# A two-part kernel on one core: another order of the first loads, and two score levels of the first unit in one product

## The chip, the cores and the metric

The kernel runs on one core of one Trainium2 chip. The metric is the device time of one execution in microseconds (us). The engines are PE (TensorE: matmuls, with PEld its weight loads), DVE (VectorE), ACT (ScalarE), POOL (GpSimd) and SP (SyncE, which here only issues DMAs).

## The reference

A recurrent attention with a decaying state feeds a mixture of four experts. All is float32.

```python
# q, k, v, alpha: (B, H, S, D) = (4, 8, 768, 48)
state = zeros(B, H, D, D)
for t in range(S):
    state = alpha[:, :, t, :, None] * state + einsum('bhd,bhe->bhde', k[:, :, t], v[:, :, t])
    y[:, :, t] = einsum('bhd,bhde->bhe', q[:, :, t], state)
x = y.transpose(0, 2, 1, 3).reshape(3072, 384)
# w1: (4, 384, 1024), w2: (4, 1024, 384), domain_probs: (3072, 4)
p = domain_probs / (domain_probs.sum(-1, keepdims=True) + 1e-9)
for e in range(4):
    out += p[:, e:e+1] * (maximum(x @ w1[e], 0) @ w2[e])
```

## The kernel before

**Units and groups.** The attention is cut into 24 units: one batch entry and 128 time steps, all 8 heads. Units are gathered into groups of two (the first) or four, and a group's 256 or 512 tokens go through the experts. The work on the experts (`up`: x times w1; `down`: the hidden layer times w2) is written out group by group and expert by expert; the generators of the attention units are stepped in between by a list of due times. The order on each engine is that of the code: the schedule is manual.

**Scores by levels.** Within a unit, the score of a query at step t with a key at an earlier step s needs the product of alpha over s+1 to t. This is done by seven levels: level li has blocks of m = 2^li steps and pairs the second half of each block pair (queries) with the first (keys). Between levels, `next_q(li)` (DVE) multiplies the queries of the second halves by the decay of the first half, `same_q(li)` (ACT) copies the others; `next_k(li)` and `same_k(li)` do the like for keys, whose first halves get the decay of the second half. `dec(li)` multiplies neighbouring decays. `QTs[li]` and `KTs[li]` are the queries and keys as level li needs them; `QTs[0]` is the query times alpha of its own step.

**The first unit** has a function of its own, `first_unit`, since nothing lies beside it. `turned` transposes an input by four TensorE products with an identity (a float32 product runs as two passes, and shows as two matmuls). `products(li, outs)` multiplies, for 4 head pairs, 2 heads and 2 halves of 64 keys, 64 keys by the 32 level-li queries of the half: 16 products. `take` (DVE) copies the masked scores of a level into `diag`. `fill` issues products with zeros into a bank that nobody reads. The tiles `QTs[1:]`, `KTs`, `plain` and `diag` lie in the buffers of the w1 pieces of later groups (`places`); the inputs of unit 1 (`apart`) and the decays lie in `spare`, which is the first of four buffers named `hT`. The other `hT` buffers are unused until `up` takes all four as `hidden`, the hidden layer of the first expert; before that, the four pieces of that expert's w2 are loaded into them.

**The first loads.** SP issues in the order of the code: unit 0's alpha, q, k, v; unit 1's alpha, k, q, v; the four pieces of the first expert's w1 (lines 1028 and 1029); unit 2's alpha, k and q after level 3's keys (line 433), into the tiles that held unit 0's; the probabilities `p_all` after the first unit (line 1043), in rows of 16 bytes; at the first `up` (line 805) the four pieces of w2; right after, four pieces of w1 and four of w2 of the second expert (lines 815 to 818 and 806). A tile that held something else waits for its readers, and each issue also waits for the eighth DMA before it to be done.

Of the kernel before, what the change touches and what calls it, by code (L numbers as in the profile page):

```python
# [10 lines left out]
F32 = mybir.dt.float32  # L11
F32R = mybir.dt.float32r
# [8 lines left out]
def kernel(  # L21
# [37 lines left out]
    nc = tc.nc  # L59
# [244 lines left out]
    def halves(t, m):  # L304
        return t.rearrange("p a (b two r) -> p a b two r", two=2, r=m)
# [7 lines left out]
    def first_unit(fill, other):  # L313
# [7 lines left out]
                       for i in range(3 * KC * QF // (NP * P))]  # L321
        place_of = iter(places)
        AT = work.tile([P, NP, P], F32, name="AT")
        QTs = [work.tile([P, NP, P], F32, name="QT")] + [next(place_of) for _ in range(6)]
        KTs = [next(place_of) for _ in range(7)]
        plain = next(place_of)
        diag, later_half = (next(place_of).rearrange("p a (i n) -> p (a i) n", i=2) for _ in range(2))
# [16 lines left out]
        def same_q(li):  # L344
            old, new = (used(t, li) for t in QTs[li:li + 2])
            nc.scalar.copy(out=new[:, :, :, 0, :], in_=old[:, :, :, 0, :])  # L346
# [25 lines left out]
        def products(li, outs):  # L372
            each = QUAD // LEVELS[li]
            qv = halves(QTs[li], LEVELS[li])
            scored(outs, KTs[li], lambda p, i, s: qv[rows[i], p, each * s:each * (s + 1), 1, :])

        def take(li, outs):
            for i in range(2):
                to = diag[:, NP * i:NP * (i + 1)]
                if li < 0:  # L380
                    nc.vector.copy_predicated(
                        to, masks_all[:, 6 * QUAD:6 * QUAD + HALF].unsqueeze(1).broadcast_to([P, NP, HALF]), outs[i])
                    continue
                m = LEVELS[li]
                mk = masks[:, li, :].rearrange("p (b r) -> p b r", r=m)
                nc.vector.copy_predicated(
                    to.rearrange("p a (b two r) -> p a b two r", two=2, r=m)[:, :, :, 1, :],
                    mk.unsqueeze(1).broadcast_to([P, NP, QUAD // m, m]),
                    outs[i].rearrange("p a (b r) -> p a b r", r=m))
# [6 lines left out]
        tq = turned(pair(rq))  # L396
        dec(0)
        nc.vector.tensor_mul(QTs[0], tq, AT)
        same_q(0)
        next_q(0)  # L400
        tk = turned(pair(rk))
        nc.scalar.copy(out=KTs[0], in_=tk)
        same_q(1)
        same_k(0)
        dec(1)
# [3 lines left out]
        fill(1, DM)  # L409
        fill(1)  # L410
        first = two("sc", HALF, tag="sc")
        products(0, part(first, 0))
        tq = turned(pair(rq))
        same_q(2)
        next_q(2)
        same_k(1)
        next_k(1)
        products(1, part(first, QUAD))
        same_q(3)
        for li in (3, 4, 5):  # L420
            dec(li)
# [8 lines left out]
        same_q(4)  # L430
        next_k(3)
        same_k(3)
        load(2, "akq")
        products(3, part(second, QUAD))
        take(0, part(first, 0))
        same_q(5)
# [358 lines left out]
    def up(gi, e, fc, slots=None):  # L795
        n = len(groups[gi]) * P
        lo, hi = (slots.start * P, slots.stop * P) if slots else (0, n)
        begins, ends = lo == 0, hi == n
        c, f = divmod(fc, FPQ)
        i = first_piece(gi, e) + c  # L800
        if fc == 0 and begins:
            for k in range(NQ):
                hidden[k] = hid.tile([P, 2, FPQ, NT], F32R, name="hT", bufs=NQ)
        if gi == fc == 0 and begins and e != 1:
            for k in range(NQ):
                load_piece(1, e * NQ + k, beside=True)
        beside = BESIDE[(gi, e) == (1, 0)]
        if fresh(gi, e) and fc in beside and begins:
            making.append(split_piece(1, first_piece(gi, e) + beside[fc]))
        if gi == 0 and e > 0 and fc in SPLIT_AT:  # L810
            making.append(split_piece(0, e * NQ + SPLIT_AT[fc]))
        if gi == 0 and e == E - 1 and fc in (3, 6):
            making.append(split_piece(1, E * NQ + 1 + fc // 3))
        if gi == 0 and e + 1 < E and fc == FCH // 2 and begins:
            for k in range(NQ if e + 1 < E - 1 else 0):
                load_piece(0, (e + 1) * NQ + k)
            for k in range(NQ if e == 0 else 0):
                load_piece(1, NQ + k, beside=True)
        col = slice(f * P, (f + 1) * P)
        if gi > 0:  # L820
            w = wt[0][i].rearrange("p t (c f) -> p t c f", f=QF)[:, :, :, col]
        else:
            w = wt[0][i].rearrange("p (c f) -> p c f", f=QF)[:, :, col]
        parts = [hidden[c][:, part, f, lo:hi] for part in range(2)]
        whole = parts[1].bitcast(F32)
        one = ps.tile([P, NT], F32, name="one", tag="g", bufs=4)[:, :hi - lo]
        if gi == 0:
            for kc in range(KC):
                nc.tensor.matmul(one, lhsT=w[:, kc], rhs=xraws[gi][:, kc, lo:hi],  # L829
                                 start=(kc == 0), stop=(kc == KC - 1))  # L830
            nc.scalar.activation(out=whole, in_=one, func=ACT.Relu)
        else:
            for part in (1, 2, 0):
                for kc in range(KC):
                    nc.tensor.matmul(one, lhsT=w[:, (0, 2, 1)[part], kc], rhs=x_part(gi, part % 2, kc)[:, lo:hi],  # L835
                                     start=(part == 1 and kc == 0), stop=(part == 0 and kc == KC - 1))
            nc.scalar.activation(out=parts[0], in_=one, func=ACT.Relu)  # L837
            while finish:
                hidden_rest(*finish.popleft())
            finish.append((one, parts))  # L840
        while finish and fc == FCH - 1:
            hidden_rest(*finish.popleft())
        background()
        if f == FPQ - 1 and ends:
            if gi == 0:
                for k in range(2 if e == E - 2 and c > 1 else 0):
                    load_piece(0, (E - 1) * NQ + 2 * (c - 2) + k)
                for k in range(NQ if e == E - 2 and c == NQ - 1 else 0):
                    load_piece(1, E * NQ + k)
                for k in range(2 if e == E - 1 and c > 1 else 0):  # L850
                    load_piece(0, E * NQ + 2 * (c - 2) + k)
            elif gi != LAST - 1:
                del wt[0][i]
                load_piece(0, i + AHEAD)
            while late:
                load_piece(1, late.popleft(), rest=True)
            while stores:
                stores.popleft()()
# [154 lines left out]
    with tc.manual_schedule():  # L1013
# [11 lines left out]

        load(0, "aqkv")
        load(1, "akqv")
        for i in range(NQ):
            load_piece(0, i)

# [3 lines left out]
        def fill(times, n=P):  # L1036
            for _ in range(times):
                nc.tensor.matmul(idle[:, :n], lhsT=zeros[:, :P], rhs=zeros[:, :n], start=True, stop=True)  # L1038
# [1 line left out]
        runs = [None, attention(1), attention(2)]  # L1040
        fill(7)
        runs[0] = first_unit(fill, runs[1])
        nc.sync.dma_start(out=p_all, in_=moe_domain_probs.rearrange("(n p) e -> p n e", p=P))

        waiting.extend(sorted([*((at, 1, runs[1]) for at in
                                 (0.4, 1.0, 2.1, 3.1, 4.4, 6.0, 7.2, 8.2, 9.2, 9.9, 10.4, 10.5, 14.4)),
                               (13.5, 2, runs[2]),
# [59 lines left out]
```

## Time and profile before

| what | us |
| --- | --- |
| three runs | 966.0, 966.89, 967.09 (median 966.89) |
| the profiled execution | 965.53 |
| its span | 963.7 |
| PE busy in it | 954.8 |
| weight loads busy | 851.9 |
| DVE, ACT, POOL busy | 534.9, 419.0, 246.2 |
| first matmul of `up` starts | 20.55 |
| first matmul of `down` starts | 26.45 |

The span is from the first to the last instruction of the profiled execution, its own time is the same execution as the device counts it. In the profile, tiles are named as in the code, but by the buffer's name where tiles share one: `w` and `w2r` are weight buffers (the first unit's `QTs`, `KTs` and `diag` show as `w`, the first expert's w1 as `w2r` or a part of `w`), `hT` the four buffers told of above, `sa`, `sk`, `sq` the tiles of alpha, k and q of units 0 and 2, `rv` the values, `tp` a bank of transposes, `sc` and `near` banks of scores, `one` and `ops` banks of `up` and `down`. "PE sc L370 x32" is then 16 products into a score bank, written at line 370. "issue" in the chain is a time in which the engine waited for nothing that the profile shows.

### The profile page before, as it was taken

Reading aid. Unit: us, or ns where it says so; the run is one execution under the profiler, and the core shown is the slowest. Engines: PE = TensorE matmul, PEld = TensorE weight load, DVE = VectorE, ACT = ScalarE, POOL = GpSimd, SP = SyncE. Lnnn points to the kernel's source line nnn. Section 1 sums busy time; section 2 is a strip of 40 time slices with the busy share of each in tenths; the row PEclk is TensorE's granted clock in tenths of the full one; section 3 lists DMA queues with packets and bytes.
Section 4 is the critical chain, followed back from the end, with each engine's and each line's share of the span. In section 5 each row is a group of like instructions: output and inputs, shape, how many; then the busy total and the mean of one; then the engine's idle time right before and its main releaser. Section 6 shows DMA issues by size and latency. Waiting matters only on the chain.

```text
span 963.7 us, 24883 instructions
## 1 busy us (share of the span) xinstructions
PE 954.8 (99%) x10252; PEld 851.9 (88%) x10252; DVE 534.9 (56%) x1127; ACT 419.0 (43%) x975; POOL 246.2 (26%) x403
## 2 busy tenths in 40 slices
PE   8999999999999999999999999999999999999998
PEld 7777779898998988989989889898898899999998
DVE  5666897778588555655645456646764312221312
ACT  5786766536445444444344333555435222021111
POOL 3121332344245222313212223223221202020200
PEclk9999999999999999999999999999999999999999
DMA  9898999999899999999999899999998609192821
GB/s 198 269 298 272 308 304 252 265 334 295 214 356 322 317 309 300 250 326 303 289 308 266 270 284 321 335 252 292 298 297 263 230 1 350 44 326 68 297 97 50
DMA packets 215618, 251.21 MB, mean 261 GB/s; under 512 B 95281, under 2 KB 184753, under 8 KB 215505
## 3 DMA queue, kind: packets, MB, share of 16 engines
q1 hardware_dynamic: 160464, 164.74, 58.3%
q0 software_dynamic: 54592, 84.55, 30.2%
q8 instruction: 81, 1.33, 0.6%
q10 hardware_dynamic: 448, 0.32, 0.1%
q14 instruction: 33, 0.26, 0.1%
HBM read 219.69 MB, written 29.88 MB: 259 GB/s over the span
## 4 chain that ended last, share of the span: by engine, by line
PE 98%; ACT 1%; issue 0%; DVE 0%; POOL 0%; DVEq 0%; POOLq 0%; ACTq 0%
PE ops L914 43%; PE one L835 38%; PE one L829 4%; PE yps L712 4%; PE sc L591 4%; PE tp L310 2%; PE sc L667 1%; PE sps L752 1%; PE sc L672 1%; PE idle L1038 0%; ACT w L346 0%; POOL lat L690 0%; PE sc L370 0%; PE y L481 0%; ACT w L355 0%
## 5 line engine op out<-in xcount | busy, mean ns | idle before, releaser
L835 PE MATMUL one<-xT,w 128*128 128x512 f32 (+1 forms) x1512 | 343.1, 383 | 0.0
L835 PEld LDWEIGHTS one<-xT,w 128*128 128x128 f32 x1512 | 271.5, 188 | 53.0 <-DVE hT L862 0.4
L914 PE MATMUL ops<-w,hT 128*128 128x384 f32 x1408 | 254.2, 338 | 0.0
L914 PEld LDWEIGHTS ops<-w,hT 128*128 128x128 f32 x1408 | 243.2, 188 | 2.5 <-issue 0.2
L837 ACT ACTIVATE hT<-one 128x512 fp32r<-128x512 f32 (+1 forms) x200 | 108.7, 547 | 280.6 <-PE one L835 279.6
L862 DVE SCALAR_TENSOR_TENSOR hT<-one,hT 128x512 fp32r<-128x512 f32 (+1 forms) x200 | 124.7, 627 | 170.6 <-ACT hT L837 170.3
L223 POOL DMA_DIRECT2D w<-in_moe_w_dram x140 | 105.8, 757 | 377.8 <-PE one L835 276.2
L914 PE MATMUL ops<-w2r,hT 128*128 128x384 f32 x704 | 127.8, 337 | 0.0
L914 PEld LDWEIGHTS ops<-w2r,hT 128*128 128x128 f32 x704 | 122.1, 188 | 0.3 <-issue 0.2
L563 ACT COPY qb<-QT 64x256 f32<-64x256 f32 x230 | 92.5, 402 | 33.0 <-DVE QT L570 31.0
L570 DVE TENSOR_TENSOR QT<-QT,AT 128x256 f32<-128x256 f32 x158 | 71.8, 455 | 33.0 <-ACT qb L563 24.7
L935 DVE SCALAR_TENSOR_TENSOR acc<-ops,p_all,acc 128x384 f32<-128x384 f32 x66 | 39.6, 612 | 86.1 <-PE ops L914 86.0
L584 DVE TENSOR_TENSOR KT<-KT,AT 128x256 f32<-128x256 f32 x161 | 76.2, 473 | 0.0
L601 DVE COPY_PREDICATED near<-masks,sc 128x128 f32<-128x128 uint8 x115 | 40.9, 355 | 62.0 <-PE sc L591 60.2
L690 POOL COPY lat<-near 32x256 f32<-32x256 f32 x92 | 45.6, 496 | 87.3 <-DVE near L601 84.0
L583 ACT COPY KT<-KT 128x256 f32<-128x256 f32 x115 | 47.2, 411 | 4.7 <-PE sc L591 2.4
L554 ACT ACTIVATE odd<-QT,ident 64x256 f32<-64x256 f32 x36 | 18.8, 523 | 69.6 <-DVE QT L512 69.3
L572 DVE TENSOR_TENSOR AT<-AT 128x256 f32<-128x256 f32 (+1 forms) x138 | 42.2, 306 | 4.7
L762 POOL TENSOR_TENSOR st<-st,dec 64x192 f32<-64x192 f32 x32 | 17.1, 535 | 95.1 <-PE yps L712 93.9
L554 ACT ACTIVATE odd<-QT 64x256 f32<-64x256 f32 x46 | 20.1, 437 | 45.0 <-DVE QT L570 44.6
L835 PE MATMUL one<-KT,w 128*128 128x256 f32 x288 | 34.6, 279 | 0.0
L835 PEld LDWEIGHTS one<-KT,w 128*128 128x128 f32 x288 | 34.4, 188 | 0.0
(135 smaller groups left out, 895.8 us busy)
## 6 DMA issues: line engine op xcount, KB each, us to landing
w<-kept SPq DMA_DIRECT2D x80, 768.0 KB, 7.4
w<-in_moe_w_dram POOLq DMA_DIRECT2D x140, 384.0 KB, 8.6
w<-kept SPq DMA_DIRECT2D x60, 384.0 KB, 6.4
w2r<-kept SPq DMA_DIRECT2D x60, 384.0 KB, 7.6
kept<-w POOLq DMA_DIRECT2D x16, 768.0 KB, 6.3
raw<-in_moe_w_dram SPq DMA_DIRECT2D x24, 384.0 KB, 9.2
kept<-w POOLq DMA_DIRECT2D x16, 384.0 KB, 8.2
kept<-w2r POOLq DMA_DIRECT2D x16, 384.0 KB, 8.2
```

Of the source, the lines that this page charges most:

```text
L223: nc.gpsimd.dma_start(out=out.rearrange("p (c n) -> p c n", c=(KC, FPQ)[l]), in_=whole_piece(l, i))
L563: nc.scalar.copy(out=qb[rows, :, i, :].rearrange("p a (b r) -> p a b r", r=m), in_=qv[rows])
L570: nc.vector.tensor_mul(qv, qv, spread(dv[:, :, :, 0], m))
L572: nc.vector.tensor_mul(dec, dv[:, :, :, 0], dv[:, :, :, 1])
L583: nc.scalar.copy(out=new[:, :, :, 1, :], in_=old[:, :, :, 1, :])
L584: nc.vector.tensor_mul(new[:, :, :, 0, :], old[:, :, :, 0, :], spread(halved(decs[li])[:, :, :, 1], m))
L601: nc.vector.copy_predicated(near.rearrange("p a (b two r) -> p a b two r", two=2, r=m)[:, :, :, 1, :], mk.unsqueeze(1).broadcast_to([P, H, ...
L690: nc.gpsimd.tensor_copy(out=lat[rows, :, rows], in_=near[rows])
L835: nc.tensor.matmul(one, lhsT=w[:, (0, 2, 1)[part], kc], rhs=x_part(gi, part % 2, kc)[:, lo:hi], start=(part == 1 and kc == 0), stop=(part ...
L837: nc.scalar.activation(out=parts[0], in_=one, func=ACT.Relu)
L862: nc.vector.scalar_tensor_tensor(out=low, in0=x, scalar=0.0, in1=top.bitcast(F32), op0=ALU.max, op1=ALU.subtract)
L914: nc.tensor.matmul(sums[slot], lhsT=h, rhs=w, start=(n == begins[slot]), stop=(n == ends[slot]))
```

## The change

The first expert's w1 is no longer loaded right behind unit 1's values. `load(2, "a")` and pieces 0 and 1 are issued when unit 0's keys have been copied, then `load(2, "k")`; `load(2, "q")` and pieces 2 and 3 follow after level 3's keys. `p_all` is loaded behind the first expert's w2, in `up`. Of this w2, piece 3 is issued before piece 2.

The products of levels 0 and 1 become one. With `KTs[1]`, even keys carry the decay of the odd step after them, so that the level-0 score of an odd query is its product with the plain query, without its own alpha. `close_q` holds the plain odd queries (`odd_q`, a copy on ACT out of the transposes' bank) and `QTs[1]` side by side, and `close_products` multiplies 64 keys by 64 queries, 16 products, with the result where the two levels' scores were. `close_q` is the second `hT` buffer, so that `hidden` now begins at the third: `hidden[2]` is `spare`, `hidden[3]` is `close_q`. Where `products(0)` stood, a fill of 384 columns is issued.

```diff
-        QTs = [work.tile([P, NP, P], F32, name="QT")] + [next(place_of) for _ in range(6)]
+        close_q = hid.tile([P, 4, NT], F32R, name="hT", bufs=NQ).rearrange("p f n -> p (f n)")
+        close_q = close_q[:, :2 * NP * P].bitcast(F32).rearrange("p (l a n) -> p l a n", l=2, n=P)
+        QTs = [work.tile([P, NP, P], F32, name="QT"), close_q[:, 1]] + [next(place_of) for _ in range(5)]
...
+        def odd_q(tq):
+            of = tq.rearrange("p a (b r two) -> p a b r two", r=2, two=2)[:, :, :, :, 1]
+            nc.scalar.copy(out=halves(close_q[:, 0], 2)[:, :, :, 1, :], in_=of)
+
+        def close_products(outs):
+            for p in range(NP):
+                for i in range(2):
+                    for s in range(2):
+                        rhs = close_q[rows[i], :, p, keys[s]].rearrange("q l (b two r) -> q l b two r", two=2, r=2)
+                        to = outs[i][keys[s], p].rearrange("q (l b r) -> q l b r", l=2, r=2)
+                        nc.tensor.matmul(to, lhsT=KTs[1][rows[i], p, keys[s]], rhs=rhs[:, :, :, 1, :],
+                                         start=True, stop=True)
...
         nc.vector.tensor_mul(QTs[0], tq, AT)
+        odd_q(tq)
         same_q(0)
         next_q(0)
         tk = turned(pair(rk))
         nc.scalar.copy(out=KTs[0], in_=tk)
+        load(2, "a")
+        for i in range(NQ // 2):
+            load_piece(0, i)
+        load(2, "k")
         same_q(1)
...
         first = two("sc", HALF, tag="sc")
-        products(0, part(first, 0))
+        fill(1, DM)
         tq = turned(pair(rq))
         same_q(2)
         next_q(2)
         same_k(1)
         next_k(1)
-        products(1, part(first, QUAD))
+        close_products(part(first, 0, HALF))
...
         same_k(3)
-        load(2, "akq")
+        load(2, "q")
+        for i in range(NQ // 2, NQ):
+            load_piece(0, i)
         products(3, part(second, QUAD))
...
         if gi == fc == 0 and begins and e != 1:
-            for k in range(NQ):
+            for k in (0, 1, 3, 2) if e == 0 else range(NQ):
                 load_piece(1, e * NQ + k, beside=True)
+            if e == 0:
+                nc.sync.dma_start(out=p_all, in_=moe_domain_probs.rearrange("(n p) e -> p n e", p=P))
...
         load(1, "akqv")
-        for i in range(NQ):
-            load_piece(0, i)
...
         runs[0] = first_unit(fill, runs[1])
-        nc.sync.dma_start(out=p_all, in_=moe_domain_probs.rearrange("(n p) e -> p n e", p=P))
```

## The prediction

> **What bounds the kernel now.** I read the page's chain of waits first, then busy time by stretches, then the chain piece by piece where TensorE idles.
>
> ```profile
> PE 98%; ACT 1%; issue 0%; DVE 0%; POOL 0%; DVEq 0%; POOLq 0%; ACTq 0%
> ...
> q8 instruction: 81, 1.33, 0.6%
> ```
>
> TensorE sets the end. Its matmuls and weight loads number 2 x 10252 = 20504; over 81 packets of queue q8 that is 253 a packet, so q8 brings TensorE's instructions, in blocks of 1.33 MB / 81 = 16 KB.
>
> ```profile
> 12.00:16.00 4.00, 2.87 (x97) 2.04 (x91) 3.48 (x13) 1.69 (x6) 0.00 (x0) 1.00 0.99 302
> 16.00:20.00 4.00, 3.16 (x113) 2.70 (x109) 3.17 (x10) 2.04 (x5) 0.19 (x1) 1.00 0.94 126
> ...
> 44.00:48.00 4.00, 4.00 (x23) 2.94 (x22) 3.36 (x9) 2.69 (x8) 0.72 (x2) 1.00 1.02 367
> ```
>
> Columns: stretch, length, then PE, weight load, DVE, ACT, POOL, the granted clock, the DMA share, GB/s. The clock is full. TensorE is idle a quarter of 12 to 20 us, and hardly again: of its 8.9 us idle (963.7 - 954.8), some 3.5 lie in the first 21 us, 0.21 + 0.35 at 33 and 36, 0.60 at 120.6, the rest after 959. So this edit can win only before 21 us, or in those small gaps. The chain there (start, length, what):
>
> ```profile
> 13.75 0.70 PE sc L370 x16
> 14.45 0.88 issue
> 15.32 0.38 PE sc L370 x10
> ...
> 16.25 0.44 PE sc L370 x27
> ...
> 17.94 1.04 PE y L481 x52
> 18.98 0.84 issue
> 19.82 0.44 PE y L481 x12
> ...
> 20.29 0.22 ACT xT L484
> ...
> 20.55 1.49 PE one L829 x11
> ```
>
> Both gaps are "issue": no semaphore, in the middle of 16 like products. Between them lie 16+16+32+4+2+4+52 = 126 matmuls with their loads, some 252 instructions: one q8 block. In 0.2 us stretches of the DMA view, q8 packets start at 13.0, 16.8 and 21.8. So I read both gaps as waits for the next code block, and the third is its like:
>
> ```profile
> 115.22 0.34 PE sps L752 x32
> 115.56 4.08 PE one L829 x18
> 119.65 1.00 PE sc L591 x67
> 120.64 0.60 issue
> 121.24 0.40 PE sc L591 x24
> ```
>
> A block seems to be asked for when the one before is entered, 126 to 128 matmuls earlier. Counting back gives 10.2, 15.32 and about 114.9, with answers at 15.32, 19.82 and 121.24: latencies of 5.1, 4.5 and 6.3 us. That is the price list for what follows.
>
> **The product.** Taken out: level 0's 16 products and level 1's 16, each 2 passes, so 64 matmuls. Put in: 16 products of 64x64 and a fill of 384 columns (2 passes): 34. So 30 matmuls and 30 loads, 60 instructions, fewer.
>
> ```profile
> 8.65 0.67 PE L370 MATMUL sc<-QT,w 64*64 64x32 f32 x32
> ...
> 9.83 0.67 PE L370 MATMUL sc<-w,w 64*64 64x32 f32 x32
> ```
>
> A 64x64 product costs what a 64x32 one does: 64 passes of levels 3 and plain, half of them of each size, took 1.16 us (18 ns each), against 0.67/32 = 21. The fill is two passes of 384 columns; four such passes of the down product took 1.29 us in the chain, so it takes 0.65. TensorE's time is a wash: -0.6 for the 32 passes, +0.65. Its second query transpose ends near 9.6 instead of 9.8, and the joint product then waits for ACT's key copy of level 0.
>
> ACT gains one copy, the odd queries out of PSUM, 128x256. No row has it. A 128x512 copy out of PSUM took 0.59 (line 394), a 128x256 one within SBUF 0.44, a 128x128 activation out of PSUM 0.28: between 0.28 and 0.59, I take 0.44, the same shape; starts overlap, so 0.33 behind 7.67. ACT's queue to 11 us slips by that: same_q(1) and same_k(0) end at 9.27 and 9.58, the joint product starts at 9.62 and ends near 10.2; level 2 runs 10.27 to 10.85, the other unit's transpose ends at 11.4, and ACT's copy of it starts at 11.55 against 11.59. ACT had 0.60 us idle before that copy, which hides the new one; without it, 0.33 would be added. DVE, full from 8 to 15.6, slips by 0.15 through same_q(1) and same_k(0), so level 4 starts at 13.90 instead of 13.75. This 0.15 hides in the code wait.
>
> **The code blocks, the term that decides.** The edge at 14.45 lies 30 matmuls later in the program: after all 32 passes of level 4 and 14 of the far product. The block behind it is asked for at 10.63 (20 passes into level 2) instead of 10.2, and by the latency of 5.1 comes at 15.75. Behind it are 34 passes in place of 64; these 64 took 1.37, so 34 take 0.7, and level 5 ends at 16.45 against 16.69: -0.25. With 4.5 it ends at 15.85 (-0.85), with 6.3 at 17.6 (+0.9). The next edge leaves the y products, 12 passes from their end, and goes 18 passes into the first up product. Without that wait, the y passes would have ended at 18.98 + 0.22 = 19.2 instead of 20.26: -1.05. So up begins at 20.55 - 0.25 - 1.05 = 19.25. It reaches the edge at 19.25 + 18 x 0.118 (42 passes took 4.96) = 21.4; the block, asked for at 15.75, is there at 20.25 by 4.5, at 22.05 by 6.3: I take no wait, at most 0.65. **Sum to here: -1.30.** Later, TensorE is full, and ACT's and DVE's work on unit 1 starts from the first up products, so it moves along.
>
> At 120.6 the edge goes to behind the 24 passes and six of `one`: reached at 120.64 + 0.40 + 1.49 = 122.5, the block being asked for about 0.45 later, so there at 121.7: **-0.60**.
>
> **The loads.** SP issues in order; what a row pays is its place.
>
> ```profile
> 8.27 2.67 SPq L258 DMA_DIRECT2D w2r<-in_moe_w_dram  x4
> 11.04 0.43 SPq L199 DMA_DIRECT2D sa<-in_alpha_dram  x1
> 11.57 1.96 SPq L199 DMA_DIRECT2D sk<-in_k_dram  x1
> 13.63 3.32 SPq L199 DMA_DIRECT2D sq<-in_q_dram  x1
> 17.00 1.87 SPq L1043 DMA_DIRECT2D p_all<-in_moe_domain_probs_dram  x1
> ```
>
> Landings, one by one: w1 pieces at 13.1, 14.1, 16.0, 17.3; unit 2's sa, sk, sq at 18.3, 19.3, 20.0; p_all 22.3; the first w2 piece 24.8. In the new order sa goes ahead of w1 0 and 1, and sk, sq ahead of w1 2 and 3. All seven are the same bytes, so the last still lands near 20.0: pieces 0 and 1 near 14 and 15 (wanted at 19.25 and 20.6), 2 and 3 near 19 and 20 (wanted at 19.25 + 4 x 0.71 = 22.1 and 23.5). Cost nothing; the cover is 3 us, each us beyond it costs one. The new waits of sa, sk, sq are on the transposes of unit 0's inputs, over by 9.6, when SP gets there at 10 or later: nothing. The w2 pieces no longer stand behind p_all, so they land some 3 us earlier, which the earlier down product (26.45 - 1.3) can use: the first had a margin of 1.65 only. Piece 2 of w2 comes last since its buffer holds unit 1's inputs and unit 0's decays, read till 20.05; behind that wait stand p_all and all of e = 1. p_all, issued at 20.3 and 5.3 us in flight, lands at 25.6; line 298 wants it at 34.77. e = 1's w1 is issued at 22.2, as before, and used at 50. Nothing.
>
> **Sum:** -1.30 - 0.60 = -1.90. Against the profiled execution, 965.53 (span 963.7 and 1.83 around it), 963.6. The runs shown have their median at 966.89, 1.36 above; so 965.0.
>
> **Rivals.**
> - *Shorter latency* (0.18). 4.5 us throughout, for the new stretch has no p_all in it: -0.85 - 1.05 - 0.60 = -2.5, 964.4. Against it: 192-byte rows of sa are now in flight as the first block is asked for.
> - *The waits only move* (0.14). 6.3 us each time: up begins at 20.55 + 0.9 - 1.05 = 20.4 and meets its block at 16.9 + 6.3 = 23.2, where it would be at 22.5: +0.55 net; with -0.60 the time is 966.8. For it: that latency came with the DMA engines full, as they are here.
> - *The gaps are no code waits* (0.05), but stay with the work, and a fill replaces the product: 966.9. Against it: the 252 instructions and the q8 packets. [...]
> - *New code waits later* (0.09). With edges 30 matmuls on, I count one block crossed in 4.8 us, from 92 to 97, where the shortest crossed without a gap took 5.6 (from 69.5). At 6.3 that costs 1.5: 966.5. Against it: the DMA share is low from 94 to 97.
> - *Slower: w1 piece 3 late* (0.12). The place is the seventh up product, which began at 24.8. If sk and sq hold SP as long as they did (1.96 and 3.32), piece 3 is issued at 16.1 and not at 12; landing took 6.8 there but up to 11.8 for this tile later on. 27.9 is 3.1 past 24.8; with -0.60, 969.4. It decides from a landing past 23.5, and the time is above the old one from 25.4 on. Against it: the engines did seven such loads by 20.0.
>
> **How the numbers follow.** The forecast has 0.42, own range 964.4 to 965.6. The time is its 965.0. The range, 963.6 to 967.3, takes in all but the slower rival and half the tail below the shorter latency. About 0.2% (1.9 us) is what a measurement tells from no change, and -1.9 is just there: half the forecast and the shorter latency are faster, 0.39, call it 0.40; of the slower rival 0.11; the rest, 0.49, is within.
>
> **What would show it.** Right: up's first product at 19.0 to 19.6; no "issue" inside the y products; a gap inside or just after the far products at about 14.7; the gap at 120.6 gone. Wrong: a gap some 18 passes into up, a wait of the fifth or seventh up product for DMA, a gap near 97, or gaps still behind the same lines.

## The result, and the profile after

| | median us | lowest to highest | executions | ratio to before |
| --- | --- | --- | --- | --- |
| before | 966.45 | 965.85 to 967.09 | 5 | |
| changed | 970.48 | 965.93 to 971.27 | 5 | 1.0036 [1.0023, 1.0049] |
| changed, taken again later | 966.3 | 965.12 to 971.62 | 12 | 1.0015 [1.0000, 1.0030] |

(Brackets are 95% intervals, each against executions of the kernel before in the same job.) By the ratios the change costs 3.5 us in the first job and 1.4 in the second, whose interval touches no change, where 1.9 us were forecast to be won. The five executions of the first job spread over 5.3 us instead of 1.2. One later execution of the kernel before, 1051.2 us at a mean clock of 0.851, is in no comparison.

The profiled execution took 971.18 us, its span 969.4 against 963.7. On its page, the chain of waits, which was TensorE almost alone, now has a DMA in it; queue q8, which brings TensorE's code, has one block less, 80 packets for 81, 16 KB each (60 instructions fewer are a quarter of a block).

```profile
PE 94%; DMA 2%; DVE 1%; ACT 1%; issue 1%; SPq 0%; POOL 0%; DVEq 0%; POOLq 0%; ACTq 0%
...
q8 instruction: 80, 1.31, 0.6%
```

What TensorE waited for (engine, line, releaser: us in total, times, the longest), first of before, then of after:

```profile
PE sc L370 <- issue: 0.9, 1, 0.9
PE y L481 <- issue: 0.8, 1, 0.8
PE sc L591 <- issue: 0.6, 1, 0.6
```

```profile
PE one L859 <- DMA w<-in_moe_w_dram: 2.4, 2, 1.7
PE sc L613 <- issue: 1.8, 2, 1.3
PE yps L734 <- issue: 1.6, 1, 1.6
...
PE far L472 <- issue: 0.4, 1, 0.4
```

The prediction reads such an "issue" as a code wait: TensorE stands at the edge of a 16 KB block of its code, and the next block has not come. The traces bear this out. In all seven waits listed, the q8 packet of the awaited block takes 1.0 to 1.5 us and ends 1.3 to 1.7 us before TensorE goes on (in after, from 12.73 to 13.69 for the wait that ends at 14.99). The three code waits of before are gone, and four others have come, with a new wait for weights. The chain of after shows where (start, length, what; "passes" below are single matmuls of the trace, two to a float32 product):

```profile
14.24 0.38 PE far L472 x13
14.62 0.37 issue
14.99 0.21 PE far L472
...
16.95 1.21 PE y L503 x64
...
18.45 4.96 PE one L853 x42
...
25.15 1.12 PE sc L613 x84
26.28 1.28 issue
27.55 0.27 PE sc L613 x7
...
35.79 1.07 PE yps L734 x30
36.86 1.59 issue
38.45 0.38 PE yps L734 x2
38.83 0.59 PE tp L310 x4
39.42 2.34 PE one L853 x12
41.76 0.85 PE tp L310 x4
42.61 3.11 PE one L853 x24
```

Up to 18.45 all went as forecast, or better: one short gap, inside the far products; none in y; `up` 2.10 us earlier than in before. Then two code waits, of 1.28 and 1.59 us. And behind the second the work itself is slow: the groups at 39.42, 41.76 and 42.61 took 2.34, 0.85 and 3.11 us where before has 1.53, 0.44 and 2.68 for them. The busy time by stretches says why (stretch, length, PE, weight load, DVE, ACT, POOL, granted clock, DMA share, GB/s):

```profile
38.00:40.00 2.00, 1.55 (x11) 1.32 (x11) 0.80 (x3) 0.78 (x3) 0.00 (x0) 0.99 0.05 12
40.00:42.00 2.00, 2.00 (x11) 2.00 (x11) 0.95 (x2) 1.46 (x5) 0.00 (x0) 0.50 0.00 0
42.00:44.00 2.00, 2.00 (x14) 2.00 (x13) 1.47 (x2) 1.53 (x5) 0.70 (x1) 0.65 0.00 0
44.00:48.00 4.00, 4.00 (x39) 4.00 (x38) 3.17 (x5) 2.30 (x7) 1.60 (x3) 1.00 0.98 379
```

The clock fell to half 1.5 us after the wait's end, for 0.04 + 2 + 1.4 = 3.4 us (a mean of 0.99, 0.50 and 0.65 over 2 us each). So around this code wait time was lost twice: once idle (1.59 us), once at half speed (2.89 - 1.28 = 1.61 us in the table below). The wait of 1.28 had no half clock behind it. PE counts as fully busy meanwhile (2.00 of 2.00 us from 40 to 42), so the busy share hides it: PE busy went up by 1.3 us with 30 passes fewer.

The balance by the same rows of work in both profiled executions (after minus before):

| row of work | before, us | after, us | difference | what came in between |
| --- | --- | --- | --- | --- |
| `up` starts | 20.55 | 18.45 | -2.10 | y wait gone, first wait short |
| first `down` goes on | 28.50 | 27.82 | -0.68 | code wait 1.28 |
| transposes after yps | 37.55 | 38.83 | +1.28 | code wait 1.59 |
| product of 12 after sps | 44.13 | 47.02 | +2.89 | half clock |
| `down` near 100 | 97.39 | 100.95 | +3.56 | code wait 0.48 |
| yps near 140 | 138.41 | 144.27 | +5.86 | before's wait at 120.6 gone, weights late 2.43 |
| end of span | 963.7 | 969.4 | +5.7 | |

What a row holds beyond the waits named is mostly the work that they break in two: the 32 passes of yps took 1.45 us for 1.08, the 27 at the late weights 3.73 for 3.23.

The loads went out as written. SP's issues (start, length, what):

```profile
8.25 0.57 SPq L199 DMA_DIRECT2D sa<-in_alpha_dram  x1
8.87 1.44 SPq L258 DMA_DIRECT2D w2r<-in_moe_w_dram  x2
10.40 0.43 SPq L199 DMA_DIRECT2D sk<-in_k_dram  x1
10.93 0.64 SPq L199 DMA_DIRECT2D sq<-in_q_dram  x1
11.62 4.81 SPq L258 DMA_DIRECT2D w2r<-in_moe_w_dram  x2
16.48 3.05 SPq L258 DMA_DIRECT2D hT<-in_moe_w_dram  x4
```

The w1 pieces landed at 15.0, 16.2, 19.6 and 20.6, and no product of `up` waited for one.

### The profile page after: what moved, and what is told of

It is laid out like the page before. It is cut to its first block, busy times and chain, and to the rows that moved or that the text cites. A ratio compares the mean times of both kernels' runs of the same rounds, so it can differ in the third digit from the quotient of the medians.

```text
span 969.4 us, 24822 instructions
## 1 busy us (share of the span) xinstructions
PE 956.1 (99%) x10222; PEld 853.0 (88%) x10222; DVE 535.2 (55%) x1127; ACT 419.8 (43%) x976; POOL 245.9 (25%) x403
## 4 chain that ended last, share of the span: by engine, by line
PE 94%; DMA 2%; DVE 1%; ACT 1%; issue 1%; SPq 0%; POOL 0%; DVEq 0%; POOLq 0%; ACTq 0%
PE ops L938 41%; PE one L859 38%; PE yps L734 4%; PE one L853 3%; PE sc L613 3%; PE tp L310 2%; DMA w<-in_moe_w_dram 2%; PE sc L689 1%; PE sps L774 1%; DMA rq<-in_q_dram 1%; PE sc L694 1%; PE idle L1060 0%; SPq L195 0%; DVE w2r L273 0%; POOL lat L712 0%
## 5 line engine op out<-in xcount | busy, mean ns | idle before, releaser
L576 ACT ACTIVATE odd<-QT,ident 64x256 f32<-64x256 f32 x36 | 18.8, 523 | 69.8 <-DVE QT L534 69.5
L734 PE MATMUL yps<-lat,rv 128*32 128x128 f32 x736 | 33.5, 273 | 1.9 <-issue 1.6
```

What stands on the lines that cost most here:

```text
L734: nc.tensor.matmul(yps[QUAD * j:QUAD * (j + 1), c, :], lhsT=lhsT, rhs=rhs, start=begins, stop=ends)
```

## The experiments

In every kernel here the outputs are computed as in the kernel before. Small idle products and held loads only add work.

### The two halves of the change

*product_alone* has the joint product and the old loads, *loads_alone* the new loads and the old products.

The diff of *product_alone* is against the changed kernel.

```diff
-        load(2, "a")
-        for i in range(NQ // 2):
-            load_piece(0, i)
-        load(2, "k")
...
+        for i in range(NQ):
+            load_piece(0, i)
...
+        nc.sync.dma_start(out=p_all, in_=moe_domain_probs.rearrange("(n p) e -> p n e", p=P))
```

> The joint product alone, all loads in the old order (w2 pieces 0, 1, 3, 2, as its buffers ask). Three theories of the changed kernel's two new code waits (1.28 us at 26.3, 1.59 us at 36.9, with a halved clock after the second). Queue: a code block waits for the data queued on the DMA engines when it is asked for, and the new load order queues more at 20 to 28 us. Then no such waits here: up starts at 19.0 to 19.6, no issue gap over 0.5 us from there to 60, time 964.5 to 966. Probabilities: it is only the 3072 small packets of p_all that stand before the block asked for at 20.4: here too no new waits, same numbers. Edges: 60 instructions fewer put the block edges where TensorE has little work between them, whatever is queued: waits at about 26 to 27 and 36 to 38, sum 2 to 3 us, time 968 to 971.

> The new order of the loads alone, with products of levels 0 and 1 apart as before (w2 pieces in order 0 to 3). Queue: blocks asked for between 20 and 28 us come 7 to 11 us later, so a gap of 0.5 to 3 us opens between 26 and 40, at the old edges (about 28 and 37); time 967.5 to 971. Probabilities: only the block asked for near 20 is late; a gap of up to 1.5 us near 28, none near 37; 966.5 to 968. Edges: no gap after 20.5 beyond those of the kernel before; 966 to 967.

*product_alone*: 967.44 us, 964.62 to 972.35, ratio 1.0015 [1.0000, 1.0031]. Its profile has one code wait of 2.69 us at 14.95, inside the far products, and half clock from 17 to 27. *loads_alone*: 964.76, 964.05 to 967.11, 0.9989 [0.9980, 0.9998]; a wait of 1.64 in level 4, none in y, `up` at 20.18, full clock. So the new loads win about 1 us, and the product alone is 1.5 us slower, with an interval that touches no change. Neither half has the long waits at 26 and 37.

### Is it one fixed place? The same kernels again

> The changed kernel itself, a second profile. If its loss is one fixed place, the gaps of 1.28 and 1.59 us at 26.3 and 36.9 are there again, with half the clock for some 4 us after 39; time 969 to 971. If the length of each wait for code varies from run to run with what the DMA engines hold, the edges lie at the same products (14.6 inside the far products, about 20.5 inside up, after some 84 of 91 score products near 26, at the end of yps near 37), but the time lost at each differs by a microsecond or more, and the times spread over 965 to 972.

> The new order of loads alone, again, beside the others of this chip. If it is faster by itself and not by luck of the first chip: 0.5 to 1.5 us under the kernel before of these runs, spread under 3 us. If its advantage was chance: no different from the kernel before, or with runs of 968 and more.

*loads_again* repeated its gain: 964.38, 963.25 to 965.85, 0.9988 [0.9979, 0.9996]. *changed_again* gave the third row of the first table, and its profiled execution (969.41 us) lost the time elsewhere than the first did. Its chain, then its stretches:

```profile
14.60 0.38 PE far L472 x13
14.98 2.43 issue
17.41 0.26 PE far L472
...
20.91 2.06 PE y L503 x64
...
23.26 6.89 PE one L853 x42
```

```profile
18.00:20.00 2.00, 2.00 (x28) 1.94 (x25) 1.19 (x5) 0.89 (x3) 0.00 (x0) 0.50 0.99 339
20.00:22.00 2.00, 2.00 (x45) 1.50 (x47) 1.06 (x2) 0.67 (x3) 0.00 (x0) 0.50 1.00 353
22.00:24.00 2.00, 1.67 (x35) 1.43 (x32) 1.93 (x5) 0.68 (x3) 0.72 (x1) 0.50 0.17 58
24.00:26.00 2.00, 2.00 (x12) 2.00 (x11) 0.57 (x2) 0.92 (x3) 0.00 (x0) 0.50 0.85 202
```

The same block edge, at the same row of work, cost 0.37 us in one execution and 2.43 in the other. Behind the long wait, the clock is halved for some 10 us: 64 y passes took 2.06 us for 1.21, 42 passes of `up` 6.89 for 4.96. No wait came at 26 or 37. So the loss isn't bound to these two places; it goes with long waits, wherever they fall.

The granted clock, which every execution lists as a mean over its span, tells the same of executions without a profile. Of the 17 of the changed kernel, 9 have 0.997 or more and 8 have 0.994 to 0.996. Eight of the first 9 took 965.12 to 966.42 us (the other is the first profiled one, 971.18 at 0.998). The 8 took 968.67 to 971.62. A mean of 0.995 over 965 us is 2 x 0.005 x 965 = 9.7 us at half clock. The 33 executions of the new loads with the old products (three kernels) have 0.998 or more.

The clock is not the whole loss. In the later job, the changed kernel's four executions at a mean clock of 1.000 took 965.14 to 966.42 us, the kernel before's seven 964.33 to 965.38. Of the gain of the new loads, in turn, more than half is clock: in the job of *loads_alone*, its nine executions at 1.000 have a median of 964.68 and those of the kernel before one of 965.17, 0.5 us apart where all executions are 1.2 apart.

### Is it what stands in the queues ahead of the code?

Counted from the start of the block ahead of it, as the prediction counts, the block awaited at 26.28 came after 7.0 us and the one awaited at 36.86 after 10.9. The first had p_all's 16-byte rows ahead of it on the DMA engines (issued at 19.57, landed at 27.47), the second the weights of the second expert (issued from 20.09 on, landed from 28.5 to 36.9). *probs_first* puts p_all ahead of w2 again (first diff). *second_later* and *loads_second_later* issue the second expert's weights about 15 us later (second diff), in the changed kernel and with the new loads alone.

```diff
+            if e == 0:
+                nc.sync.dma_start(out=p_all, in_=moe_domain_probs.rearrange("(n p) e -> p n e", p=P))
             for k in (0, 1, 3, 2) if e == 0 else range(NQ):
                 load_piece(1, e * NQ + k, beside=True)
-            if e == 0:
-                nc.sync.dma_start(out=p_all, in_=moe_domain_probs.rearrange("(n p) e -> p n e", p=P))
```

```diff
-        if gi == 0 and e + 1 < E and fc == FCH // 2 and begins:
+        if gi == 0 and e + 1 < E and (fc == FCH // 2 and begins if e else fc == 0 and not begins):
```

> The changed kernel, but p_all is loaded ahead of the first expert's w2 instead of behind it. Probabilities: the gap at 26.3 falls to under 0.3 us and with it the one at 36.9, no halved clock, time 964.5 to 966. Queue: p_all holds SP back for some 3 us as in the kernel before, so the first gap shrinks; the second expert's eight pieces are still queued when the next block is asked for near 27, so a gap of 0.5 us or more near 37 stays; 966 to 970. Edges: both gaps stay as they are, 969 to 971.

> The changed kernel, but the second expert's eight pieces are issued at the start of the second part of the first up stage (after about 37 us) instead of at 20 to 30. Queue: with p_all and w2 alone on the DMA engines, the blocks asked for at 20.4 and 26 to 28 come within 5 us: no gap over 0.5 us from 25 to 40, clock full, up at 18.5 to 19.5, time 963.5 to 966 unless the pieces come too late for 50. Edges: the gap at 26 stays (only 5.8 us of work in that block), the one at 37 shrinks; 966.5 to 969.

> The new order of loads alone (products of levels 0 and 1 apart), and the second expert's eight pieces issued after 37 us. Queue: a little under the loads alone, 963.8 to 965.0, from earlier code blocks behind 20 us; slower than it, up to 967, if the pieces are late for the second expert's up products at 50 or for their split. Edges: the same as the loads alone, 964.3 to 965.3.

*probs_first*: 968.59, ratio 1.0027 [1.0009, 1.0045]; waits of 1.59 at 14.92 and, with p_all long landed, 1.55 at 29.34, at the edge in the scores where the changed kernel had 1.28. So p_all's rows are not what makes that wait. *second_later*: 969.21, 1.0045 [1.0022, 1.0069]; no long wait near 26 or 37, but 1.94 at 14.89, and later transfers of keys and of weights late by 2.1 and 3.4. *loads_second_later*: 968.93, 1.0035 [1.0014, 1.0057], with a code wait of 1.24 and 1.9 of late keys and queries near 64: the later weights hurt by themselves. About the second expert's weights as a queue these two runs say little, since the waits at 26 and 37 were absent from *changed_again* as well, where nothing was moved.

*after_held* and *loads_held* were to keep the DMA engines free while the first block is fetched: a DMA of one row, which must wait for the products that read its target, holds SP, and w1 pieces 0 and 1 and the keys come behind it.

```diff
-        for i in range(NQ // 2):
-            load_piece(0, i)
-        load(2, "k")
...
+        nc.sync.dma_start(out=QTs[1][:1, 0, :D], in_=alpha[0, 0, :1, :])
+        for i in range(NQ // 2):
+            load_piece(0, i)
+        load(2, "k")
```

> The changed kernel, with SP held until the joint product is done (a DMA of one row of 48 into a tile that this product reads, issued behind unit 2's alpha); w1 pieces 0 and 1 and unit 2's k go behind it. So when the second code block is asked for, at about 10.3, only two loads, landing by 12.2, are queued. Queue: the block comes within 4 us, the gap at 14.6 is under 0.2 us, and the clock stays full to 20. The later gaps may stay. Time 1 to 3 us under the changed kernel. If the time of a code fetch doesn't hang on the data that is queued: a gap of 0.4 to 2.7 us in the far products as in the other runs.

> The new order of loads with the products of levels 0 and 1 apart, SP held in the same way until level 1's products are done (about 10). Queue: the gap inside level 4, 1.64 us in the loads alone, falls under 0.4 us, up starts at 18.5 to 19.3; 963 to 964.5. Otherwise: the gap stays at 0.9 to 1.7 us and the time within 0.5 us of the loads alone.

*after_held*: 967.32, 965.17 to 969.91, 1.0017 [1.0007, 1.0027], with a wait of 1.72 in the far products where under 0.2 was expected. But the engines were not free. SP came past the hold at 10.15 and issued the two pieces then (8.87 in the changed kernel), just as the block is asked for at about 10.2, and unit 1's inputs were still in flight (the DMA share is the number before the last):

```profile
9.00:11.00 2.00, 2.00 (x73) 1.72 (x71) 1.93 (x9) 1.74 (x6) 0.00 (x0) 1.00 1.12 221
11.00:12.00 1.00, 1.00 (x62) 0.91 (x64) 1.00 (x4) 0.80 (x3) 0.00 (x0) 1.00 0.63 124
```

So this run doesn't tell whether a queue ahead of the block makes the first wait long. The changed kernel's first profile gives a hint that it can. If a block is asked for when the one ahead is entered, the q8 packets of two blocks in a row were asked for at 27.55 and 38.45. The one began at 35.63, after 8.1 us of full DMA engines, the other at 39.64, after 1.2 us of empty ones:

```profile
27.50:35.60 8.10, 7.67 (x97) 5.09 (x96) 5.12 (x16) 3.54 (x11) 1.49 (x4) 1.00 1.01 335
38.40:39.60 1.20, 1.15 (x9) 0.92 (x8) 0.44 (x2) 0.38 (x2) 0.00 (x0) 1.00 0.01 1
```

It is no more than a hint: in *loads_held*, a packet asked for at 14.34 began at 16.39, only 2.1 us later, with the engines as full (a share of 1.08).

*loads_held* had the first wait fall to 0.23, as the queue's side expected, but *loads_again* has 0.32 there without a hold, and `up` began at 19.84, later than the 19.3 expected. *loads_held* is the best version found, 964.23 (963.93 to 965.54), 0.9983 [0.9974, 0.9992], faster than both kernels; it can't be told from the new loads alone. Its chain has the pair of waits of before, where before had them:

```profile
13.41 0.70 PE sc L370 x16
14.11 0.23 issue
14.34 0.38 PE sc L370 x10
...
16.95 1.04 PE y L488 x52
17.99 1.12 issue
19.11 0.44 PE y L488 x12
...
19.84 4.96 PE one L838 x42
```

### Is it the place of the edges, or the joint product?

Seven kernels put TensorE's instruction count back, or moved it, with small idle products in place of fills:

```diff
-        fill(1)
+        for _ in range(17):
+            nc.tensor.matmul(idle[:HALF, :QUAD], lhsT=zeros[:HALF, :HALF], rhs=zeros[:HALF, :QUAD], start=True, stop=True)
         first = two("sc", HALF, tag="sc")
-        fill(1, DM)
```

This is *edges_30*. *edges_16* has 9 of them and *edges_62* 34 at this place; *edges_back* has 18 for three of the seven first fills, *edges_mid* 16 ahead of level 4, in the changed kernel. *before_shifted* has 16 ahead of level 4 in the kernel before, *loads_edges_30* 17 with the new loads alone.

> The changed kernel with 18 small idle products (64x64 zeros by 32 columns) in place of three of the seven first fills: 60 instructions more ahead of the first transpose, in about the same time, so that the block edges lie at the same products as in the kernel before. Edges: gaps as in the kernel before (about 0.9 inside level 4, 0.8 inside the y products), none after 20.5; 965 to 967. Queue and probabilities: the two early gaps come back, and a block asked for between 19 and 28 is still late: a gap of 0.5 us or more between 26 and 40; 967.5 to 971.

> The changed kernel with the fill ahead of level 4 (two passes of 384 columns, 0.65 us, in a gap of TensorE) written as 16 small idle products (64x64 by 32 columns, 32 passes, 0.56 us): 60 instructions more at no cost of time, so that all block edges from level 4 on lie at the same products as in the kernel before. (The run edges_back was to do this at the start of the kernel, where its small products took 0.11 us each and 2.7 us in all.) Edges: a gap inside level 4, perhaps one inside the y products, none over 0.5 us from 21 to 60; like the new loads alone: 964 to 966. Queue: a block asked for between 19 and 28 still comes late and a gap over 0.5 us between 26 and 40 stays, 967 to 971.

> The kernel before, with the same writing of the fill ahead of level 4 as 16 small products: 60 instructions more from there on, loads and products as before. If code edges are worth microseconds by themselves, the edges 30 passes earlier change the time by more than 0.5 us either way with nothing else changed: the first gap stays inside level 4 or moves ahead of it, the second comes at the start of the y products. Edges: 964 to 969, not 966. Queue: within 0.5 us of the kernel before, 965.5 to 966.5.

> The changed kernel with two of the three fills ahead of the joint product (four passes, 0.87 us) written as 17 small ones (34 passes, 0.6 us): 60 instructions more before the first block edge, so that every edge, and the point where each block is asked for, lies at the same product as in the kernel before. Edges alone decide: first gap inside level 4, second in the y products, each under 1.6 us, no half clock in most runs; like the new loads alone, 964 to 965.5, spread under 3 us. The joint product loses in another way: 966 to 970 as the changed kernel beside it.

> The changed kernel with one fill of 384 columns ahead of the joint product written as 9 small ones: 32 instructions more, first edge two passes before the end of level 4, second a few passes into up. Edges alone decide: between edges_30 and the changed kernel, and different from both if the place counts; one gap of 0.5 to 2.5 us near 14.5, 964.5 to 969. Another way: as the changed kernel.

> The changed kernel with all three fills ahead of the joint product (six passes) written as 34 small ones (68 passes, about 1.2 us): 124 instructions more; the first edge moves ahead of level 4, among the plain products near 12, where TensorE has 1.5 us of fill and idle time behind it; the second falls in the first half of the y products. Edges alone decide: a gap near 12 of 1 to 3 us, of which 0.8 is free, another in the y products; 965 to 970, not the time of edges_30. Another way: as the changed kernel.

> The kernel with the new loads alone, its two fills ahead of level 0 (four passes) written as 17 small ones (34 passes): 60 instructions more, first edge ahead of level 4. Edges alone decide: it loses what made it fast, a gap of 1 to 2.5 us near 12 to 13, half the clock behind it in many runs, 966 to 970. If the edges don't count: 964 to 965 as the new loads alone.

| kernel | median us | ratio | passes, us they took |
| --- | --- | --- | --- |
| edges_back | 972.24 | 1.0061 [1.0043, 1.0080] | 36, 4.05 |
| edges_mid | 968.78 | 1.0031 [1.0019, 1.0043] | 32, - |
| before_shifted | 970.41 | 1.0053 [1.0034, 1.0073] | 32, - |
| edges_30 | 969.31 | 1.0037 [1.0023, 1.0051] | 34, 2.17 |
| edges_16 | 965.84 | 1.0000 [0.9987, 1.0013] | 18, 1.23 |
| edges_62 | 970.90 | 1.0047 [1.0031, 1.0063] | 68, 4.15 |
| loads_edges_30 | 970.18 | 1.0042 [1.0029, 1.0055] | 34, 2.33 |

These are spoiled. A pass of these idle products took 61 to 69 ns (64 in *edges_30*, 2.17 / 34), and 112 in *edges_back*, where one of the score products takes 18 to 21. So the joint product, which stands behind them, began 0.7 us (*edges_16*) to 3.2 us (*edges_back*) later than in the changed kernel. And in *edges_62* the clock was halved from 12.0 to 18.8 with no code wait ahead of it. They don't say what an edge costs. *edges_16*, which disturbs least, lost nothing against before.

The last two kernels use products whose time is known. *edges_same* is the changed kernel with level 0's old 16 products back in their old place, in place of a fill (the joint product writes over their result). It has TensorE's instruction count, and so every edge, of the kernel before. *loads_edges_32* has the new loads and the old products, with level 0's issued twice and a fill less: the edges come 30 passes earlier in the work.

```diff
         first = two("sc", HALF, tag="sc")
-        fill(1, DM)
+        products(0, part(first, 0))
```

```diff
-        fill(1, DM)
         fill(1)
         first = two("sc", HALF, tag="sc")
-        products(0, part(first, 0))
+        for _ in range(2):
+            products(0, part(first, 0))
```

> The changed kernel, with the 384-column fill ahead of unit 0's second query transpose replaced by the kernel before's own 16 products of level 0 (32 passes in about 0.65 us; their result is written over by the joint product, so it is idle work). TensorE then has exactly as many instructions as before, and every block edge stands at the same row of work as before: inside level 4 and inside the y products. If it is the edges' places that cost (theory), the waits are as with the new loads alone (together 0.6 to 1.7 us, up's first product at 19.2 to 20.2, clock full) and the median is 0.9 to 1.9 us under the kernel before (ratio 0.998 to 0.999). If it is the joint product itself, or the moved work around it (rival), the first wait stays 1.4 to 2.7 us, and the ratio is 1.001 to 1.003.

> The new loads alone, with level 0's 16 products issued twice and the 384-column fill ahead of them left out (32 passes for 2, about the same 0.65 us; what is computed stays the same). The edges then stand 30 passes earlier in the work: at the start of level 4, and 30 passes earlier in the y products. If the edges' places matter (theory), the waits differ from those of the new loads alone: the first block is asked for 0.4 us earlier and reached 0.5 us earlier, so the waits are as long as there to 0.2 us, and the ratio is 0.998 to 1.000. If the loads alone gain because of where their edges happen to stand (rival), this kernel loses 1 us or more against them: ratio 1.000 to 1.003.

*edges_same*: 965.21, 963.39 to 967.0, ratio 0.9991 [0.9982, 1.0001]. *loads_edges_32*: 966.36, 965.2 to 972.89, 1.0017 [0.9999, 1.0034]. The joint product with the old edges stands where the new loads do, though its interval just touches no change, and none of its 11 executions goes over 967.0, where 9 of the changed kernel's 17 do. The old products with other edges lose the gain of the new loads (their interval lies above that of *loads_alone*) and scatter as the changed kernel does: there, the rival's number came true, that the new loads gain only with the edges where before has them. Both sides say that it is where the edges fall, each by one kernel. Not all went as expected: the profiled execution of *edges_same* has one wait, at the old place, but with half clock behind it (transposes 1.04 for 0.59), and `up` begins at 20.97, later than the 20.2 allowed for:

```profile
13.49 0.70 PE sc L372 x16
14.19 1.11 issue
15.30 0.38 PE sc L372 x10
...
17.27 1.04 PE tp L310 x4
...
19.48 1.21 PE y L503 x64
```

And the profiled execution of *loads_edges_32* is its fastest, with waits of 0.99 (levels 3 and plain) and 0.62 (y) and `up` at 19.93: where its long executions lose was not seen. One of these took 969.5 us at a mean clock of 1.000, so half clock isn't needed for a loss.

## Why the prediction failed

**What was right.** The count: 30 passes and 30 weight loads fewer (10222 against 10252). That the gaps are block edges: they moved with the count, to the very pass named (after 14 far passes), and the first came back with it in *edges_same*. No gap in y, none 18 passes into `up`, the gap at 120.6 gone. The product as a wash: joint product and fill in the place of two products cost nothing that *edges_same* could tell from the new loads alone (0.9991 [0.9982, 1.0001] against 0.9983 to 0.9989). ACT's copy of the odd queries took 0.41 (0.44 taken) and was hidden. `up` started at 18.45, 0.8 earlier than the 19.25 forecast, since level 4 began at 13.30 and not 13.90, and its block came at 14.99 and not 15.75. That the wait there was as short as 0.37 was luck of this execution: at the same edge, the five other traces with the joint product and the changed kernel's edges show 1.59 to 2.69. The loads: w1 landed at most 1.2 us after the forecast, so the slower rival (w1 piece 3 late) did not happen. p_all was 1.9 us later than forecast, without a price.

**The step that failed** is the one called "the term that decides". It priced each block at 4.5 to 6.3 us from request to arrival, from three blocks of one execution, and wrote: "That is the price list for what follows." The request itself is in no trace: that a block is asked for when the one ahead is entered was the author's estimate. The awaited packets of before and after begin 1.6 to 8.1 us behind that entry. Counted in the same way, the blocks that the changed kernel's first profile waited for took 4.8 (10.2 to 14.99), 7.0, 10.9 and 5.4 us; in *product_alone*, *probs_first*, *changed_again* and *after_held* the first one took 7.1, 6.0, 6.9 and 6.2. With the new loads and the old products, it took 4.5 to 5.9. The sum had -1.30 for this stretch; the profile after had -2.10 by `up` and then +3.35 of new waits (1.28 + 1.59 + 0.48). "Later, TensorE is full" was the sentence that left these out. The rival "New code waits later" was of the right kind, but looked for them at 92 to 97 alone and gave them 1.5 us (the one that came there, at 99.86 in after, cost 0.48). Of the others, "The waits only move" names 966.8, but no trace shows its two waits, and none of the 17 executions lies between 966.42 and 968.67; "The gaps are no code waits" is out, since *edges_same* puts the gap back at its old row by the count alone.

**The term that was missing** is the clock. The prediction read it as full in the one profile of before, and priced a wait by its length. In the kernels without small idle products, 8 of the 12 code waits of over 1 us had half clock from near their end on (from 1.11 in *edges_same* to 2.69 in *product_alone*), and 4 had not (1.12 in *loads_held*, 1.28 in the changed kernel, 1.55 in *probs_first*, 1.64 in *loads_alone*). That the wait brings it about is likely by this, and not shown. In *changed_again*, one wait of 2.43 us, 0.7 more than the two of before together, went with half clock from 17.1 to 27.3 and put `up` behind by 2.7 us at its start (23.26 against 20.55) and by 4.6 after its 42 first passes (6.89 us for 4.96).

In the traces, 1.00 and 0.50 are the only steady values of the clock. The half stretch was 3.4 us in the changed kernel (from 40.0 to 43.4), 6.8 in *edges_62* (from 12.0 to 18.8) and 10.2 in *changed_again* and *product_alone*, and executions of one kernel split into groups by their mean clock (of the changed kernel's 17, 8 have 0.994 to 0.996, 9 have 0.997 or more). What sets the length of a half stretch, and when one begins, no run shows.

**The weights at 138 to 143** (2.4 us) were in no step. The three transfers they waited for were issued 3.5 us later than in before (127.17 against 123.66), as all work was by then. But lateness isn't the cause: *changed_again* issued them at 128.31, later still, and had no wait, since they landed 9.1 to 9.6 us after issue, where the first profile took 11.6 to 16.4 and before 9.6 to 10.1. *loads_again*, which issued them early, at 122.30, took 12.3 to 16.1 and waited 1.4 us at full clock. So these transfers vary from execution to execution, with the change and without it. Whether the change makes long transfers more frequent was not tested, and why they take so long stays open.

**Open.** Why a block that is reached at another place of the work is so often slower to come. P_all and the joint product were each tried and are each out as the single cause. What else stands in the DMA queues is not: the runs that were to move it either failed to (*after_held*) or can't be told from chance (*second_later*). What the traces show is where the time goes. The q8 packet itself takes 0.9 to 2.5 us and ends 1.2 to 1.8 us before TensorE goes on, in every code wait of every kernel here; the rest, which varies, lies before the packet begins. That it hangs on where the edge falls rests on *edges_same* and *loads_edges_32*; by what, the runs don't say.

## What to carry to other kernels

Before removing or adding instructions ahead of a part where TensorE just keeps up with its code, count instructions to the next 16 KB edges, and allow for a code arrival that varies by several us, as here (4.0 to 10.9). In *changed_again*, a wait of 2.4 us with half clock behind it put the work 4.6 us behind. Test such an edit with a twin that has the same instruction count as the kernel before (idle products whose time is known from the trace); the twin separates what the edit does from where it moves the edges. Run the parts of a change alone: here the loads' order was worth 1.1 to 1.6 us by itself (ratios 0.9989 to 0.9983), and with the old products it beats the kernel before, as the changed kernel does not.

## What the hardware showed that was not expected

- Where TensorE waited for it, a code block took 4.0 to 10.9 us from the start of the block ahead of it, which is read here as its request, to its own start. The same edge of the same kernel cost 0.37 us in one execution and 2.43 in another.
- The kernel before pays for its clock too: in one job, its 7 executions at a mean clock of 1.000 took 964.33 to 965.38 us, the 27 others (0.996 to 0.999) 965.03 to 968.29.
- Small idle products of 64x64 by 32 columns took 61 to 69 ns a pass (112 in *edges_back*) where the score products of that size take 18 to 21. They all wrote to one place; that this is the reason was not tested. Half clock began without a code wait ahead of it right behind them in *edges_62* (from 12.0 to 18.8) and while they ran in *loads_edges_30* (from 9.1 to 19.4).
- The same three weight transfers landed 9.1 to 9.6 us after issue in one execution of the changed kernel and 11.6 to 16.4 in another.
